# A gated linear-attention block and a bilinear FFN on one core: weights assembled as integers, and the order of the beginning

## The chip, the core and the metric

The kernel runs on one core of a Trainium2 chip. A core has TensorE (PE: matrix products), VectorE (DVE), ScalarE (ACT), GpSimd (POOL) and SyncE (SP), each with an instruction queue of its own that is worked off in order; they wait for each other through semaphores. The metric is the device time in microseconds, as the median of three runs.

## The reference

Four sequences (B = 4) of 768 tokens with 8 heads of 48 channels go through a gated recurrence, and its output through a bilinear feed-forward layer:

```python
f = 1.0 / (1.0 + np.exp(-f_logit))
for t in range(S):
    state = f[:, :, t, :, None] * state + np.einsum('bhd,bhe->bhde', k[:, :, t], v[:, :, t])
    y[:, :, t] = np.einsum('bhd,bhde->bhe', q[:, :, t], state)
x = y.transpose(0, 2, 1, 3).reshape(B * S, H * D)      # 3072 x 384
out = (x @ w_a) * (x @ w_b) @ w_out                    # 384 -> 1536 -> 384
```

q, k, v and f_logit are float32. The weights are float64: w_a, w_b and w_out reach the kernel as raw 64-bit words, 14 MB in all.

## The kernel before

**Attention.** The work is cut into 16 units: four heads and 384 tokens (BLK) each. Units 0 and 1 make the first block of 384 tokens (block 0), units 2 and 3 the second (block 1). A unit's f, k, q and v stand in one of three sets of buffers; unit 3 reuses unit 0's set. `front(u)` prepares a unit: ScalarE takes two sigmoids of f, one for `inv` and one in place; POOL scales `inv`; VectorE scans the running products of f and of the reciprocal gates (L242, L252) and multiplies them into q and k (L253, L254). These generators advance one step with each `next`. Then, on TensorE: `scores(u)` (24 products of k and q, masked by VectorE at L299), `turn(u)` (six transposes of k, copied by ScalarE as kT at L312), `within(u)` (scores times v), `gains(u)` (k times v; VectorE sums them into states, L343 and L345), `across(u)` (states times q). ScalarE copies y from PSUM at L396, and five DMAs move it into xT, the transposed input of the feed-forward layer (L410). y has one buffer only, so the next unit's copies wait for these DMAs.

**Feed-forward.** `up(blk, ft)` multiplies one block with 128 columns of w_b and of w_a: 3 + 3 matrix products, shown as x6 + x6 rows, L426. `product()` then lets ScalarE copy the b half (L441) and VectorE multiply it with the a half (L446). `down` multiplies three blocks of tokens with w_out in seven products instead of eight; its rows are L478 and L483.

**Weights.** The weights come in 20 pieces of up to 768 columns a partition: w_b and w_a alternate, then w_out. `load_weights` starts a piece's DMA into one of four raw buffers. `from_double` makes float32 of it, with two handles: `begin(n)` runs the first part of pieces up to n, `end(n)` the last. In the first part ScalarE takes the absolute value of the high words (scaled, so that the exponent fits), their sign, and the sign as a bit; POOL limits the value. The last part is four passes on VectorE (L188, L192, L194, L195), which shift the value into place, join the sign, cut out the power of two, scale the low words by it and add them. `up(0,0)` needs the first pieces of w_b and w_a, and the program makes its second product wait for the following w_b piece too; the later ups follow in the same manner.

**Order.** The whole program stands under a manual schedule: each engine takes its instructions in the order of the calls. From "with tc.manual_schedule()" on, the beginning is written out by hand, up to `up(0, 4)`; then the list `rest` begins with `up(1, 0)` and goes on in a loop, with the later units' parts queued beside it. Loads of all kinds and most xT DMAs leave through SP's queue, the others of the first two units through ScalarE's.

Of the kernel before, what the change touches and what calls it, by code (L numbers as in the profile page):

```python
# [78 lines left out]
def by_quotients(ctx, tc, q, k, f_logit, v, moe_w_a, moe_w_b, moe_w_out, out, ident, weights, bad):  # L79
# [7 lines left out]
    NJ = BLK // SUB  # L87
    NTG = BLK // 128
    NU = B * NH * NQ
    NBLK = B * NH  # L90
    NSET = 3

    fixedp = ctx.enter_context(tc.tile_pool(name="fixed", bufs=1))
# [21 lines left out]
    ones = fixed([128, 1], "ones")  # L115
    less = fixed([128, 1], "less")
    sign = fixedp.tile([128, PIECE], BF16, tag="sign", name="sign")
    bits = [fixedp.tile([128, PIECE], U32, tag=f"bit{i}", name=f"bit{i}") for i in range(3)]
# [7 lines left out]
    def load_unit(u, names="fkqv"):  # L126
        if u >= NU:
            return
        b, half, qd = unit(u)
        t = sets[u % NSET]  # L130
        cols = slice(half * BLK, half * BLK + BLK)
        for nm, src in (("f", f_logit), ("k", k), ("q", q)):
            if nm not in names:
                continue
            heads = src[b].rearrange("(n two) d s -> two d n s", two=2)
            for par in range(2):
                nc.sync.dma_start(out=t[nm][R * par:R * par + D], in_=heads[par][:, 2 * qd:2 * qd + 2, cols])
        if "v" in names:
            nc.sync.dma_start(
                out=t["v"].rearrange("s n c x -> s n (c x)"),  # L140
                in_=v[b, 2 * qd:2 * qd + 2, :, half * NC:half * NC + NC].rearrange("n s c two d -> s n (c two d)"),
            )

    def pieces():
# [5 lines left out]
        for ft in range(0, NFT, 2):  # L150
            rows = moe_w_out[ft * 128:(ft + 2) * 128]
            yield w_out[:, ft:ft + 2], rows.rearrange("(k p) c -> p k c", p=128), (2, DM)

    todo, raws, going = list(pieces()), [], []
    ended = [0]

    def load_weights(n=1):
        for _ in range(n):
            if len(raws) == len(todo):
                return  # L160
            dst, src, (k, m) = todo[len(raws)]
            raw = dst
            if src.dtype != FP32:
                raw = raw_pool.tile([128, PIECE], mybir.dt.uint64, tag="raw", name="raw")[:, 0:k * m]
                raw = raw.rearrange("p (k m) -> p k m", k=k)
            nc.sync.dma_start(out=raw, in_=src)
            raws.append(raw)

    def from_double(dst, raw, k, bit):


# [6 lines left out]
        bit, sgn = bit[:, 0:width], sign[:, 0:width]  # L178
        nc.scalar.activation(h, hi.bitcast(FP32), AF.Abs, scale=HI_SCALE)  # L179
        nc.scalar.activation(sgn, hi.bitcast(FP32), AF.Sign)  # L180

        nc.scalar.activation(
            bit.bitcast(U16).rearrange("p (n two) -> p n two", two=2)[:, :, 1], sgn, AF.Relu, scale=-32768.0
        )
        nc.gpsimd.tensor_scalar(h, h, HI_MAX, None, ALU.min)  # L185
        yield
        hu = h.bitcast(U32)
        nc.vector.scalar_tensor_tensor(  # L188
            out=hu, in0=hu, scalar=3, in1=bit, op0=ALU.logical_shift_left, op1=ALU.bitwise_or
        )  # L190

        nc.vector.tensor_scalar(bit, hu, 0xFF800000, None, ALU.bitwise_and)  # L192
        h, lo, power = (x.rearrange("p (k n) -> p k n", k=k) for x in (h, lo, bit.bitcast(FP32)))
        nc.vector.scalar_tensor_tensor(out=dst, in0=lo, scalar=2.0**-52, in1=power, op0=ALU.mult, op1=ALU.mult)  # L194
        nc.vector.tensor_tensor(dst, h, dst, ALU.add)  # L195
        yield

    def begin(n):

        while len(going) < min(n, len(todo)):  # L200
            i = len(going)
            dst, src, shape = todo[i]
            going.append(from_double(dst, raws[i], shape[0], bits[i % len(bits)]) if src.dtype != FP32 else iter(()))
            next(going[i], None)

    def end(n):

        while ended[0] < min(n, len(todo)):
            begin(ended[0] + 1)
            next(going[ended[0]], None)  # L210
            ended[0] += 1
            if ended[0] > 2:
                load_weights()
# [8 lines left out]

    live = {}
    xT = {}

# [3 lines left out]
    def front(u):  # L229

        t = sets[u % NSET]
        x = halves(t["f"])
        inv = sb2.tile([128, 2 * BLK], FP32, tag="inv", name="inv")
        nc.scalar.activation(inv, x, AF.Sigmoid, bias=less, scale=-1.0, accum_out=tails[:, u:u + 1])  # L234
        nc.scalar.activation(x, x, AF.Sigmoid)

# [3 lines left out]
        for n in range(2):  # L240
            c = slice(n * BLK, n * BLK + BLK)
            nc.vector.tensor_tensor_scan(x[:, c], x[:, c], none, math.exp(MIDDLE), ALU.mult, ALU.add)  # L242
        nc.vector.tensor_tensor(held[:, u], t["f"][:, :, BLK - 1], least, ALU.is_ge)
        yield

        start = sb2.tile([128, 2, NC - 1], FP32, tag="start", name="start")
        nc.vector.reciprocal(start, t["f"].rearrange("p n (c m) -> p n c m", m=C)[:, :, 0:NC - 1, C - 1])  # L247
        for n in range(2):
            for c in range(NC):
                w = slice(n * BLK + c * C, n * BLK + c * C + C)  # L250
                first = start[:, n, c - 1:c] if c else math.exp(-MIDDLE)
                nc.vector.tensor_tensor_scan(inv[:, w], inv[:, w], none[:, 0:C], first, ALU.mult, ALU.add)  # L252
        nc.vector.tensor_tensor(halves(t["q"]), halves(t["q"]), x, ALU.mult)  # L253
        nc.vector.tensor_tensor(halves(t["k"]), halves(t["k"]), inv, ALU.mult)  # L254
# [62 lines left out]
    def gains(u):  # L317
# [19 lines left out]
        before = live[u - NQ]["st"][NJ] if half else None  # L337
        live[u]["st"] = [before]
        for j in range(NJ - 1 if last else NJ):
# [6 lines left out]
            before = st[:, j]  # L346
            live[u]["st"].append(before)
        if not last:

            for n in range(2):  # L350
                end = t["f"][:, n, BLK - 1:BLK]
                nc.vector.tensor_scalar(before[:, n], before[:, n], end, math.exp(-MIDDLE), ALU.mult, ALU.mult)
# [19 lines left out]
    def across(u):  # L372
# [22 lines left out]
        for p, e, r, rows in (*whole, (1, R, 0, D), (1, 0, R, D)):  # L395
            nc.scalar.copy(y[r:r + rows, :, p], ps[p][e:e + rows, 0:BLK].rearrange("r (o m) -> r o m", m=SUB))  # L396
        y = y.rearrange("r (n c) p m -> r n (c p m)", n=2)
# [17 lines left out]

    HFT = NFT // 2
    products = {}
# [108 lines left out]
    def slot(u):  # L526
# [18 lines left out]
        yield  # L545
        next(nxt, None)
        yield

# [15 lines left out]

    with tc.manual_schedule():
        nc.scalar.preload_act_table_set("sigmoid_and_others")
        for x, value in ((less, -K_EXP), (zero, 0.0), (least, math.exp(MIDDLE - DECAY_MAX)), (ones, 1.0)):
            nc.gpsimd.memset(x, value)
        for n, x in (("f", 30.0), ("k", 0.0), ("q", 0.0)):
            for u in range(NSET):  # L570
                eng = nc.vector if n == "f" or n == "q" and u == 0 else nc.gpsimd
                eng.memset(sets[u][n], x)
        for ps in (ps_x, ps_y):
            nc.scalar.copy(ps[:, :, 0:BLK], zero.unsqueeze(1).broadcast_to((128, 2, BLK)))
        load_unit(0, "f")
        load_unit(1, "f")
        load_unit(0, "kqv")
        load_unit(1, "kqv")
        load_weights(2)
        load_unit(2)  # L580
        load_weights(2)


        fronts = [front(u) for u in range(2 * NQ + 1)]
        next(fronts[0])
        next(fronts[1])
        for bit in bits:
            nc.gpsimd.memset(bit, 0)
        make_identity(nc, ident)
        nc.gpsimd.memset(causal, 1.0)  # L590
        for p in range(2):
            half = causal[SUB * p:SUB * p + SUB]
            nc.gpsimd.affine_select(
                out=half, in_=half, compare_op=ALU.is_ge, fill=0.0, base=0, pattern=[[1, SUB]], channel_multiplier=-1
            )
        next(fronts[0])
        next(fronts[0])
        next(fronts[1])
        scores(0)
        turn(0, True)  # L600
        begin(2)
        next(fronts[1])
        within(0)
        gains(0)
        next(fronts[2])
        scores(1, True)
        turn(1, True)
        across(0)
        within(1, True)
        end(1)  # L610
        gains(1)
        across(1)
        for u in range(NQ):
            load_unit(u + NSET)
            load_weights()
        end(2)
        begin(3)


        next(fronts[2])  # L620
        next(fronts[2])
        scores(2)
        turn(2, True)
        next(fronts[3])
        begin(4)
        within(2)
        end(3)
        gains(2)
        up(0, 0)
        across(2)  # L630
        next(fronts[3])
        product()
        end(4)
        begin(5)
        up(0, 1)
        next(fronts[3])
        product()
        begin(6)
        scores(3)
        turn(3, True)  # L640
        up(0, 2)
        within(3)
        end(5)
        gains(3)
        product()
        end(6)
        begin(8)
        across(3)
        up(0, 3)
        product()  # L650
        up(0, 4)

# [16 lines left out]

        queue = [(2 * NFT - 4 + d, fronts[2 * NQ]) for d in (0, 0.9, 1.8)]  # L670
        for s in slots:
# [405 lines left out]
```

## Time and profile before

| what | us |
|---|---|
| median of 3 runs (lowest, highest) | 654.95 (654.27, 656.79) |
| the profiled execution, its span | 657.89, 656.1 |
| TensorE busy | 618.1 (94%) |
| VectorE busy | 327.7 (50%) |
| ScalarE busy | 174.9 (27%) |
| POOL busy | 68.9 (10%) |
| granted TensorE clock, mean over the span | 0.981 |

In the profile, a row of the timeline gives the start in the span, the time taken, the engine and the line, what was written from what, how many instructions are merged into it, and in brackets how long the engine had been idle before it and what ended that. The rows of slices give, for 40 equal stretches of the span, the busy tenths of each engine and the granted clock of TensorE in tenths. A window's row gives the busy time of each engine in a stretch, with the number of instructions, and the mean granted clock. A row named DMA_DIRECT2D is the issue of a transfer, not the transfer; the trace also has the time at which it landed.

### The profile page before, as it was taken

The numbers are of one execution on the slowest core, as the hardware profiler recorded it, in microseconds if no ns is written. First come the engines' busy times: TensorE is split into PE (matmuls) and PEld (weight loads), VectorE is DVE, ScalarE is ACT, GpSimd is POOL, SyncE is SP. The second block draws the span as 40 slices with busy tenths as digits, with TensorE's granted clock in tenths as the row PEclk, the third lists the DMA queues.
The fourth block names the chain that finished last, engine by engine and source line by source line (L and its number), as shares of the span: only waits on it lengthen the run. The fifth ranks groups of instructions, "written<-read, shape, count | busy, mean of one in ns | idle before, by whom it ended". The sixth has DMA issues, their size and how long they took to land.

```text
span 656.1 us, 12293 instructions
## 1 busy us (share of the span) xinstructions
PE 618.1 (94%) x5202; PEld 446.9 (68%) x5202; DVE 327.7 (50%) x610; ACT 174.9 (27%) x312; POOL 68.9 (10%) x57
## 2 busy tenths in 40 slices
PE   1667899999999999999999999999999999999996
PEld 1554555557898666966699666865689655865696
DVE  7878699995875345351443244443363121311241
ACT  3564677531321222122200312122200122011100
POOL 6232365410110000000000000000000000000000
PEclk9966999999999999999999999999999999999999
DMA  8688556100144124040210033140000000000000
GB/s 209 172 207 238 164 169 221 68 0 1 37 106 116 37 55 91 15 104 1 63 32 35 25 79 71 22 115 0 20 1 24 26 19 19 0 26 0 1 24 30
DMA packets 30209, 43.37 MB, mean 66 GB/s; under 512 B 3776, under 2 KB 24768, under 8 KB 30144
## 3 DMA queue, kind: packets, MB, share of 16 engines
q1 hardware_dynamic: 29856, 42.19, 23.7%
q8 instruction: 43, 0.70, 0.5%
q10 hardware_dynamic: 288, 0.30, 0.2%
q14 instruction: 22, 0.18, 0.1%
HBM read 33.03 MB, written 4.72 MB: 58 GB/s over the span
## 4 chain that ended last, share of the span: by engine, by line
PE 90%; DVE 5%; DMA 2%; ACT 1%; issue 1%; POOL 0%; ACTq 0%; SPq 0%; DVEq 0%
PE f L426 57%; PE f L483 24%; PE ps_x L283 2%; PE ps_y L363 2%; PE ps_y L384 2%; PE ps_x L329 1%; DMA xT<-y 1%; DVE inv L252 1%; PE ps_x L310 1%; DVE f_in L242 1%; PE f L310 1%; DVE k_in L254 1%; DMA f_in<-in_f_logit_dram 0%; DVE h L478 0%; DVE q_in L253 0%
## 5 line engine op out<-in xcount | busy, mean ns | idle before, releaser
L426 PE MATMUL f<-xT,w_a 128*128 128x384 f32 x576 | 203.6, 490 | 5.6 <-DVE start L247 4.6
L426 PE MATMUL f<-xT,w_b 128*128 128x384 f32 x576 | 205.7, 494 | 0.0
L426 PEld LDWEIGHTS f<-xT,w_a 128*128 128x128 f32 x576 | 110.1, 191 | 83.2 <-issue 6.4
L426 PEld LDWEIGHTS f<-xT,w_b 128*128 128x128 f32 x576 | 107.8, 191 | 70.4 <-issue 1.2
L446 DVE TENSOR_TENSOR ab<-f,b_sb 128x384 f32<-128x384 f32 x96 | 53.0, 554 | 180.4 <-PE f L426 130.1
L441 ACT COPY b_sb<-f 128x384 f32<-128x384 f32 x96 | 46.0, 479 | 238.9 <-PE f L426 225.8
L483 PE MATMUL f<-raw,h 128*128 128x192 f32 x432 | 73.7, 328 | 0.0
L483 PEld LDWEIGHTS f<-raw,h 128*128 128x128 f32 x432 | 70.2, 190 | 0.5
L483 PE MATMUL f<-w_out,ab 128*128 128x192 f32 x288 | 51.1, 327 | 0.9 <-DVE u L478 0.9
L237 POOL TENSOR_SCALAR inv<-inv 128x768 f32<-128x768 f32 x16 | 16.3, 1020 | 328.1 <-ACT inv L234 328.1
L185 POOL TENSOR_SCALAR h<-h 128x768 f32<-128x768 f32 (+1 forms) x20 | 44.0, 2202 | 61.3 <-ACT h L179 61.3
L483 PEld LDWEIGHTS f<-w_out,ab 128*128 128x128 f32 x288 | 47.4, 190 | 3.0 <-DVE u L478 1.2
L478 DVE TENSOR_TENSOR o<-f,u 128x192 f32<-128x192 f32 x36 | 12.9, 357 | 56.6 <-PE f L483 56.4
L283 PE MATMUL ps_x<-q_in,k_in 48*64 48x64 f32 x720 | 16.2, 238 | 22.1 <-DVE k_in L254 22.1
L283 PEld LDWEIGHTS ps_x<-q_in,k_in 48*64 48x64 f32 x720 | 14.6, 151 | 23.9 <-POOL causal L590 13.9
L242 DVE TENSOR_TENSOR_SCAN f_in<-f_in,zero 128x384 f32<-128x384 f32 x32 | 28.8, 941 | 3.1 <-POOL inv L237 3.1
L299 DVE TENSOR_TENSOR at<-ps_x,causal 128x768 f32<-128x768 f32 x15 | 14.4, 958 | 31.4 <-PE ps_x L283 31.3
L252 DVE TENSOR_TENSOR_SCAN inv<-inv,start,zero 128x128 f32<-128x128 f32 x64 | 27.5, 470 | 0.0
L345 DVE TENSOR_TENSOR st<-st,ps_x 128x96 f32<-128x96 f32 x80 | 20.3, 253 | 12.1 <-PE ps_x L329 9.6
L483 PE MATMUL f<-raw,ab 128*128 128x192 f32 x144 | 25.7, 328 | 0.0
L483 PE MATMUL f<-w_out,h 128*128 128x192 f32 x144 | 25.4, 326 | 0.0
L396 ACT COPY y<-ps_y 48x384 f32<-48x384 f32 (+1 forms) x45 | 21.4, 475 | 11.1 <-PE ps_y L384 10.0
(82 smaller groups left out, 477.1 us busy)
## 6 DMA issues: line engine op xcount, KB each, us to landing
f_in<-in_f_logit_dram SPq DMA_DIRECT2D x32, 144.0 KB, 3.2
k_in<-in_k_dram SPq DMA_DIRECT2D x32, 144.0 KB, 3.6
q_in<-in_q_dram SPq DMA_DIRECT2D x32, 144.0 KB, 3.9
v_in<-in_v_dram SPq DMA_DIRECT2D x16, 288.0 KB, 4.2
raw<-in_moe_w_out_dram SPq DMA_DIRECT2D x6, 768.0 KB, 4.3
out_dram<-o SPq DMA_DIRECT2D x24, 192.0 KB, 1.9
raw<-in_moe_w_b_dram SPq DMA_DIRECT2D x5, 768.0 KB, 7.4
raw<-in_moe_w_a_dram SPq DMA_DIRECT2D x5, 768.0 KB, 6.2
```

The lines of the kernel that those rows point to most:

```text
L185: nc.gpsimd.tensor_scalar(h, h, HI_MAX, None, ALU.min)
L237: nc.gpsimd.tensor_scalar(inv, inv, EXP_K, 1.0, ALU.mult, ALU.add)
L242: nc.vector.tensor_tensor_scan(x[:, c], x[:, c], none, math.exp(MIDDLE), ALU.mult, ALU.add)
L252: nc.vector.tensor_tensor_scan(inv[:, w], inv[:, w], none[:, 0:C], first, ALU.mult, ALU.add)
L283: nc.tensor.matmul(ps[h][SUB * p:SUB * p + SUB, o:o + SUB], lhsT=kf[r, tokens(n, c, p)], rhs=qf[r, tokens(n, c, p)], start=True, stop=True,)
L299: nc.vector.tensor_tensor(to, x, tri.broadcast_to((128, *lead, 2 * NC, SUB)), ALU.mult)
L345: nc.vector.tensor_tensor(st[:, j], before, new, ALU.add)
L396: nc.scalar.copy(y[r:r + rows, :, p], ps[p][e:e + rows, 0:BLK].rearrange("r (o m) -> r o m", m=SUB))
L426: nc.tensor.matmul(ps[nm], lhsT=w[:, kt, ft * 128:ft * 128 + 128], rhs=x[:, kt], start=kt == 0, stop=kt == NKT - 1,)
L441: nc.scalar.copy(b_sb, ps["b"])
L446: nc.vector.tensor_tensor(products[blk, part][:, :, i], a, b, ALU.mult)
L483: nc.tensor.matmul(to, lhsT=x[:, i], rhs=w[:, i], start=first and i == 0, stop=i == HFT - 1, skip_group_check=True)
```

## The change

It has four parts.

1. The low word of a double is no longer added in float32. ScalarE turns it into an integer-valued float in [2^23, 2^24] (one more pass: Identity with a scale of 2^-29 and a bias of 2^23), so that its bits hold the rounded low mantissa bits; the sign pass then overwrites that word's upper half with the sign bit. VectorE shifts the high value left by three and adds the two as 32-bit integers: two passes instead of four. In the built program the add is an instruction of its own kind, over twice as many 16-bit elements. `begin` can now run half of a piece's first part (`begin(4.5)`).
2. f of units 0 and 1 is loaded over all 64 rows of each half of the buffer (16 rows of the next head fill the rest), and needs no memset before it. The products of f of these two units stand in a buffer of their own, borrowed from the pool `ab`. POOL fills f with 30.0 before units 3 and 4 are loaded.
3. The raw words of pieces 4 and 5 go to two free buffers of the pool `ab`.
4. The beginning is reordered: the order of the loads (v late, k of unit 0 after the first w_b piece), `begin(3)` ahead of `scores(0)`, `turn` before `across` and `scores` of units 0 and 1, and unit 2 after `up(0,0)` instead of before it. Two of unit 0's and 1's y copies go to VectorE. `front`'s multiplications of q and k are a step of their own.

```diff
+    EARLY = (4, 5)
...
+                if len(raws) in EARLY:
+                    raw = ab_pool.tile([128, NTG * HFT * 128 // 2], mybir.dt.uint64, tag="ab", name="ab")
...
     def load_unit(u, names="fkqv"):
...
+        if u - NSET in FIRST and "f" in names:
+            nc.gpsimd.memset(t["f"], 30.0)
...
+            if nm == "f" and u in FIRST:
+                for par in range(2):
+                    row = ((b * H + 4 * qd + par) * D) * S + half * BLK
+                    rows = bass.AP(src.tensor, src.offset + row, [[S, R], [2 * D * S, 2], [1, BLK]])
+                    nc.sync.dma_start(out=t[nm][R * par:R * par + R], in_=rows)
...
     def from_double(dst, raw, k, bit):
...
         nc.scalar.activation(h, hi.bitcast(FP32), AF.Abs, scale=HI_SCALE)
+        nc.scalar.activation(bit.bitcast(FP32), lo, AF.Identity, bias=whole, scale=2.0**-29)
+        nc.gpsimd.tensor_scalar(h, h, HI_MAX, None, ALU.min)
+        yield
         nc.scalar.activation(sgn, hi.bitcast(FP32), AF.Sign)
...
-        nc.gpsimd.tensor_scalar(h, h, HI_MAX, None, ALU.min)
         yield
         hu = h.bitcast(U32)
-        nc.vector.scalar_tensor_tensor(
-            out=hu, in0=hu, scalar=3, in1=bit, op0=ALU.logical_shift_left, op1=ALU.bitwise_or
-        )
-        nc.vector.tensor_scalar(bit, hu, 0xFF800000, None, ALU.bitwise_and)
-        h, lo, power = (x.rearrange("p (k n) -> p k n", k=k) for x in (h, lo, bit.bitcast(FP32)))
-        nc.vector.scalar_tensor_tensor(out=dst, in0=lo, scalar=2.0**-52, in1=power, op0=ALU.mult, op1=ALU.mult)
-        nc.vector.tensor_tensor(dst, h, dst, ALU.add)
+        nc.vector.tensor_scalar(hu, hu, 3, None, ALU.logical_shift_left)
+        hu, bit = (x.rearrange("p (k n) -> p k n", k=k) for x in (hu, bit))
+        nc.vector.tensor_tensor(dst.bitcast(U32), hu, bit, ALU.add)
...
+            copy = nc.vector.tensor_copy if u in FIRST and p else nc.scalar.copy
...
```

The new beginning, without the memsets and with the lines of the old one left out:

```python
        load_unit(0, "f")
        load_unit(1, "f")
        next(fronts[0])
        load_unit(1, "q")
        load_unit(0, "q")
        load_unit(1, "k")
        load_weights()
        load_unit(0, "k")
        load_weights()
        patterns()
        next(fronts[0])
        load_weights()
        next(fronts[0])
        load_unit(1, "v")
        next(fronts[1])
        next(fronts[1])
        next(fronts[0])
        load_unit(0, "v")
        next(fronts[1])
        begin(3)
        load_unit(2, "k")
        load_unit(2, "f")
        scores(0)
        load_unit(2, "v")
        next(fronts[1])
        turn(0, True)
        within(0)
        gains(0)
        load_unit(NSET, "f")
        load_weights()
        next(fronts[2])
        turn(1, True)
        across(0)
        load_weights()
        scores(1, True)
        end(2)
        within(1, True)
        load_unit(2, "q")
        gains(1)
        across(1)
        load_weights()
        next(fronts[2])
        next(fronts[3])
        end(3)
        next(fronts[2])
        up(0, 0)
        next(fronts[2])
        load_unit(NSET, "q")
        begin(4.5)
        load_weights()
        product()
        load_unit(NSET, "v")
        end(4)
        scores(2, True)
        up(0, 1)
        next(fronts[3])
        load_unit(NSET + 1, "q")
        end(5)
        load_unit(NSET, "k")
        end(6)
        within(2)
        load_unit(NSET + 1, "f")
        load_unit(NSET + 1, "k")
        turn(2, True)
        load_weights()
        gains(2)
        load_unit(NSET + 1, "v")
        next(fronts[3])
        next(fronts[3])
        product()
        begin(7)
        up(0, 2)
        product()
        across(2)
        up(0, 3)
        begin(8)
        scores(3)
        turn(3, True)
        within(3)
        gains(3)
        across(3)
        up(0, 4)
        end(7)
        product()
        product()
        end(8)
```

## The prediction

> **What bounds the kernel now.** First the page's rows of slices, 16.4 us each.
>
> ```profile
> PE   1667899999999999999999999999999999999996
> DVE  7878699995875345351443244443363121311241
> ACT  3564677531321222122200312122200122011100
> PEclk9966999999999999999999999999999999999999
> ```
>
> TensorE is the bound from the fifth slice on; before it, it idles while VectorE is nearly full, and its granted clock falls in slices 3 and 4. The timeline of TensorE says where its work stands.
>
> ```profile
> 13.91 1.68 PE L283 MATMUL ps_x<-q_in,k_in 48*64 48x64 f32 x48 [13.91 <-DVE k_in L254]
> ...
> 37.81 1.65 PE L283 MATMUL ps_x<-q_in,k_in 48*64 48x64 f32 x48 [7.97 <-DVE k_in L254]
> ...
> 43.27 2.65 PE L426 MATMUL f<-xT,w_b 128*128 128x384 f32 x6
> ...
> 55.41 4.18 PE L426 MATMUL f<-xT,w_a 128*128 128x384 f32 x6 [4.60 <-DVE start L247]
> ...
> 82.48 2.10 PE L426 MATMUL f<-xT,w_a 128*128 128x384 f32 x6
> ```
>
> 13.91 is scores(0), 37.81 scores(2), 43.27 up(0,0); the pair ending in the last row is up(1,0), done at 84.42. I use 84.42 as the checkpoint: all work after it has the same order in both kernels. The third row with a wait names L247, but the VectorE row just before it is L195, the last pass of a weight piece (54.30 to 55.26): that is what this up waited for. The windows split the time at those marks:
>
> ```profile
> 30.00:35.00 5.00, 0.00 (x0) 0.00 (x0) 4.86 (x12) 1.89 (x4) 0.00 (x0) 0.56 0.04 10
> 40.00:45.00 5.00, 5.00 (x97) 3.99 (x96) 4.83 (x8) 4.45 (x8) 2.02 (x2) 0.58 1.07 293
> 55.00:60.00 5.00, 4.37 (x10) 2.04 (x11) 5.00 (x11) 1.70 (x2) 2.24 (x1) 0.50 0.56 121
> ...
> 43.27:84.42 41.15, 34.09 (x313) 20.62 (x311) 30.22 (x49) 23.73 (x34) 14.79 (x8) 0.86 0.77 211
> 84.42:150.00 65.58, 65.58 (x205) 38.68 (x204) 63.99 (x83) 38.56 (x55) 25.95 (x13) 1.00 0.32 104
> ```
>
> (PE, PEld, DVE, ACT, POOL busy, then clock.) From 84.42 on TensorE has no idle time to win, though VectorE is full; everything is decided before. There TensorE is idle 7.06 us of 41.15 and runs at half clock in two stretches (0.50 to 0.58 in the rows).
>
> **Part 1, weights as integers.** Four VectorE passes become two. The old ones, of the piece that ended the 4.60 us wait, and the new ScalarE pass's nearest row:
>
> ```profile
> 51.23 0.95 DVE L188 SCALAR_TENSOR_TENSOR h<-h,bit 128x768 uint32<-128x768 uint32 x1
> 52.22 1.06 DVE L192 TENSOR_SCALAR bit<-h 128x768 uint32<-128x768 uint32 x1
> 53.31 0.96 DVE L194 SCALAR_TENSOR_TENSOR w_a<-raw,bit 128x768 f32<-128x768 uint32 x1
> 54.30 0.96 DVE L195 TENSOR_TENSOR w_a<-h,w_a 128x768 f32<-128x768 f32 x1
> ...
> 43.16 0.89 ACT L179 ACTIVATE h<-raw 128x768 f32<-128x768 f32 x1
> ```
>
> From 51.23 to 55.18 is 3.95 us, in other pieces 3.43. New: a shift, nearest row L192 (usually 0.56), 0.59 with the step to the next; and an integer add, which no row shows. Its nearest row is L195, 0.96. Against the change speaks the Trainium skill, "DVE: scalar operands, raw-bit mode, write accounting and state across instructions", Raw-bit mode: the lane's add is fp32, exact on raw integers only below 2^24. So a 32-bit add must go in halves, and the built program indeed writes a 256-column piece as 512 columns. Twice 768 elements at L195's rate would be about 1.8 us. I take 0.96, with 1.8 as the other end: a piece costs 1.55 (or 2.4) instead of 3.43. At 1.8 the sum below loses some 0.5 us (up(0,1)), since the other pieces stand under matmuls.
>
> ScalarE gets a fourth pass, start to start 0.8: 3.6 us a piece instead of 2.8, and 2.05 for half pieces. Later, each up has one piece and one b_sb copy: 3.13 + 0.82 = 3.95 us of ScalarE (82.68 to 85.81 in the trace, plus the pass) per 3.87 of TensorE. For 11 piece-equivalents that is under 1 us of lag; a copy may come 1.9 us late before its product does, so it costs nothing.
>
> **Part 2, f whole and loads reordered.** The first f load left at 1.74, behind VectorE's memset; ScalarE and POOL start at 0.79, so I take 0.85. SP's loads land one after another: 0.68 us per 48-row load (issued 3.60 to 5.01, landed 7.20 to 9.36), v 1.0, half weight pieces 1.3, whole ones 2.0. The f loads grow to 64 rows, 0.9 each. In the new order: f of both units 6.5, q1, q0, k1 10.5, w_b 11.8, k0 13.2, w_a 14.5, w_b's second piece 16.6, v1, v0 18.6, k2, f2 21.3, v2, f3 23.7, w_a's second piece 25.8. VectorE has finished f0's and f1's scans and unit 0's quotients by 12.0, but k0 lands at 13.2: its product ends at 14.1 and scores(0) starts at 14.3. Nothing is won at the first matmul; the gain of the early f is used up by k0's place in the queue.
>
> **Part 3, the reordered beginning, step by step.** begin(3) puts three pieces on ScalarE ahead of unit 0's two kT copies: w_b 11.8 to 13.9, w_a 14.5 to 16.6, then 3.6 to 20.2. The copies end at 21.1 (17.58 before), and gains(0) ends 21.75 (19.49 before). VectorE's state chain takes 1.75 (rows L343, L345): 23.6; turn(1) and across(0) end 24.6. The y copies, shared with VectorE, end 26.3; scores(1)'s masks 27.2; within(1), gains(1) 29.6; states 31.4; across(1) 31.6, against 29.85 now. Here the change is 1.8 us behind.
>
> Then it gains. Now the second y waits 4.89 us for the first y's DMAs (ScalarE L396) and is done at 34.1; then it is ready at 32.8. Its ScalarE-issued xT DMAs leave until 33.9 and land 3.0 later (the last one now took 3.04), 37.0. up(0,0) runs from 37.2 instead of 43.27; but unit 2's four steps, which stand before it now, come after. VectorE, meanwhile: f2's scans 34.5, a piece 36.2, quotients 38.5, q2 and k2 40.3. Those hide in up(0,0).
>
> TensorE's sum from 37.2 to the end of up(1,0): six ups at 3.87 (a clocked-up pair, 80.55 to 84.42), 23.2; units 2 and 3, each scores 0.86, turn 0.75, within 0.8, gains 0.67, across 0.82: 7.8; less 1.3 of up(0,0) that runs early, on the first third of xT: 29.7. Waits: kT2 0.7, unit 3's mask and states 0.6; up(1,0), now only one up behind across(3) instead of two. Its xT needs 1.5 us of copies, five SP issues at 0.6 and 2.1 to land: across(3) ends about 63, ready 68.8, TensorE there 67.6, so 1.2. Together 2.5.
>
> Clock: TensorE idles from 31.6 to 37.2 and starts slow. The Trainium skill, "TensorE: Matmul & The Clock Gate", What's actually happening, has full rate return after about 3.4 us of sustained work, which at half speed loses 1.7. The rows say longer: work resumed at 37.81 and 55.41, the clock rose near 44.2 and 64.7, so 6.4 and 9.3 us, the second with a 0.2 us gap in it. Up(0,0) is dense, so I take 5.5 us, a loss of 2.8; by the rule the result would be 1.1 us lower, by the longer row 1.9 higher.
>
> 37.2 + 29.7 + 2.5 + 2.8 = 72.2, against 84.42: 12.2 us. The profiled execution took 657.89 (span 656.1, 1.8 around it), the median of the runs is 654.95; executions differ by that much, and I take the gain off the median: 654.95 - 12.2 = **642.8**.
>
> The two weight pieces loaded early, into product buffers that are free then, cost nothing: their raw words land about 31 and 37 (47.55 and 53.86 before), and ScalarE reaches them at 40 and 44. up(0,2), at 49.4, waits for the first of them, put together by 48.9; landing 10 us later it would eat that cover and hold up(0,2) by some 0.5. POOL loses three bit memsets (2.09 us) and gets three f memsets of 0.7, idle around both. The split step of each unit's front runs its halves in succession later on: nothing.
>
> **The rivals.** (1) The new chain slips: kT0 stands behind a weight load that must land at 16.6, and xT behind DMAs that share engines with weight loads (one now took 8.08 us behind them). 2 to 4 us late moves all: 645 to 647. (2) The clock stays low: a gap in each window, at scores(2), kT2 or the states, as at 59.8. Half clock until about 52 would lose 7.5 instead of 2.8: 647.5. For it speaks the 9.3 us case; against it, VectorE has slack at each of those points. (3) Slower: ScalarE becomes the bound. Should the new pass, integer in and strided, cost not 0.82 but x, each later step takes 3.13 + x against 3.87. With 11 pieces there, six more ahead of copies in the beginning and some 2 us that buffers absorb, 17(x - 0.74) - 2 reaches 12.2 at x = 1.6; at 2.0 the kernel would take about 662. The rows of L179 and L180 with the same stride (0.89) speak against it. (4) It does nothing: early waits merely move, and up(1,0) ends where it does now, 655. Against it, 5 us of waits and 5 of half clock have named causes here that go.
>
> **How the numbers follow.** Expected course 0.68, (1) 0.14, (2) 0.09, (4) 0.05, (3) 0.04. A measurement tells about 0.5% (3.3 us) from no change: below 651.7 lie the first three, 0.91; 0.05 within; 0.04 slower. The likeliest's own range is 639.5 to 645.5 (clock 1.9 up or 1.1 down, chain 1 to 2 either way); with (1) and most of (2) it reaches to 648.5.
>
> **What would show it.** scores(0) near 14; kT0 copied only after 20; across(1) ending after 31; up(0,0) at about 37 at half clock, full clock by 44; no TensorE wait of over 2 us between 40 and 72; up(1,0) done near 72; the integer add near 1 us and the new Identity pass near 0.85; from there the same rows, 12 us earlier. Wrong it would be with loads landing later than 0.68 us apart, a long wait at kT0 or xT, or ScalarE setting the pace of the ups.

## The result: 649.3 us, less than half of the gain that was predicted

The changed kernel takes 649.33 us (median of 4 runs, 648.95 to 650.63) against 654.80 before: a ratio of 0.9914, 95% interval 0.9889 to 0.9940. The forecast was 642.8, its range ended at 648.5. A later measurement gave 648.74 (6 runs, 647.99 to 650.09) against 657.01 for the kernel before, ratio 0.9879 (0.9857 to 0.9902); that too lies outside the range. The kernel after repeats well; the kernel before scatters from 654.3 to 658.7, and the gain with it, from 5.5 to 8.3 us.

The profiled execution took 649.68 us (span 647.9). The page's rows of slices, as shown for before:

```profile
PE   0859899999999999999999999999999999999996
DVE  6778345587774427161642345352444021311241
ACT  6577599632221322211201222122200212011100
PEclk9969999999999999999999999999999999999999
```

TensorE now has its idle time and its slow clock in the first slices alone; VectorE's full stretch is gone (busy 289.7 us instead of 327.7), ScalarE has more to do there (187.0 instead of 174.9). The timeline of TensorE for the same steps:

```profile
15.56 1.68 PE L308 MATMUL ps_x<-q_in,k_in 48*64 48x64 f32 x48 [15.56 <-DVE start L271]
...
38.12 1.65 PE L451 MATMUL f<-xT,w_b 128*128 128x384 f32 x2 [5.62 <-DVE w_b L211]
40.91 1.62 PE L451 MATMUL f<-xT,w_b 128*128 128x384 f32 x2 [1.15 <-DMA xT<-y]
42.32 4.04 PE L451 MATMUL f<-xT,w_a 128*128 128x384 f32 x6
46.29 0.93 PE L308 MATMUL f<-q_in,k_in 48*64 48x64 f32 x48
...
74.75 0.88 PE L451 MATMUL f<-xT,w_b 128*128 128x384 f32 x2 [0.51 <-DMA xT<-y]
75.47 2.10 PE L451 MATMUL f<-xT,w_a 128*128 128x384 f32 x6
```

15.56 is scores(0); 31.59 (not shown) to 46.29 is up(0,0), cut in three by waits; scores(2) follows it. The last row is the end of up(1,0), so the checkpoint lies at 77.40, the start of the next row; 72.2 was predicted, 84.42 stood before. The 4.60 us wait in the middle of up(0,1) is gone. The long waits are now inside up(0,0): 5.62 us for the third piece of weights, then 1.15 us for the last part of xT. The windows (PE, PEld, DVE, ACT, POOL busy, then clock):

```profile
35.99:46.23 10.24, 6.96 (x10) 3.03 (x10) 7.09 (x13) 9.54 (x13) 5.69 (x3) 0.50 1.00 308
46.23:77.40 31.17, 28.89 (x441) 18.34 (x441) 20.43 (x40) 18.64 (x29) 7.54 (x5) 1.00 0.70 179
77.40:150.00 72.60, 72.60 (x276) 43.39 (x275) 40.49 (x62) 49.52 (x71) 27.57 (x14) 1.00 0.33 105
```

One stretch at half clock instead of two, just over up(0,0), and full clock from there on.

Why up(0,0) came late is told by VectorE's and ScalarE's timelines around the second y and by the DMA view of 24 to 42 us (last column: median us from issue to landing):

```profile
33.43 1.14 DVE L422 COPY y<-f 48x384 f32<-48x384 f32 x2 [1.74 <-DMA xT<-y]
34.60 1.81 DVE L266 TENSOR_TENSOR_SCAN f_in<-f_in,zero 128x384 f32<-128x384 f32 x2
...
36.52 0.55 DVE L209 TENSOR_SCALAR h<-h 128x768 uint32<-128x768 uint32 x1
37.11 0.96 DVE L211 CUSTOM_DVE_ANT_0 w_b<-h,bit 128x1536 uint16<-128x1536 uint16 x1
```

```profile
33.40 0.97 ACT L422 COPY y<-f 48x384 f32<-48x384 f32 x2 [7.72 <-DMA xT<-y]
34.66 1.81 ACTq L436 DMA_DIRECT2D xT<-y  x3
```

```profile
xT<-y SPq DMA_DIRECT2D x4, 72.0 KB, 2.2
...
xT<-y ACTq DMA_DIRECT2D x2, 72.0 KB, 4.9
xT<-y ACTq DMA_DIRECT2D x2, 48.0 KB, 2.2
xT<-y ACTq DMA_DIRECT2D x2, 24.0 KB, 5.1
```

The second y waits for the DMAs of the first (one buffer), and they are late: SP issues the load of piece 4 at 27.68, ScalarE its last xT transfer at 28.23; the load lands at 33.05, the 24 KB transfer at 33.30. The same happens again: piece 5's load issued at 35.25, the last xT transfer (72 KB) at 35.85; they land at 40.45 and 40.78. In this execution the transfers issued ahead of the weight loads took 2.2 us (the rows of 72 KB on SP's queue and of 48 KB). The shift and the integer add of a piece are the two rows at 36.52 and 37.11.

### The profile page after: what moved, and what is told of

The parts are those of the page before. It is cut to its first block, busy times and chain, and to the rows that moved or that the text cites. A ratio compares the mean times of both kernels' runs of the same rounds, so it can differ in the third digit from the quotient of the medians.

```text
span 647.9 us, 12250 instructions
## 1 busy us (share of the span) xinstructions
PE 614.6 (95%) x5202; PEld 442.0 (68%) x5202; DVE 289.7 (45%) x572; ACT 187.0 (29%) x328; POOL 65.6 (10%) x58
## 4 chain that ended last, share of the span: by engine, by line
PE 92%; DMA 4%; ACT 1%; SPq 1%; DVE 0%; ACTq 0%; issue 0%; DVEq 0%
PE f L451 58%; PE f L508 26%; DMA xT<-y 2%; PE ps_y L409 2%; PE ps_y L388 2%; PE ps_x L354 2%; PE ps_x L308 2%; PE ps_x L335 1%; DMA q_in<-in_q_dram 1%; DMA raw<-in_moe_w_a_dram 1%; SPq L145 0%; PE f L335 0%; ACTq L436 0%; DVE y L422 0%; ACT bit L204 0%
## 5 line engine op out<-in xcount | busy, mean ns | idle before, releaser
L261 POOL TENSOR_SCALAR inv<-inv 128x768 f32<-128x768 f32 x16 | 18.0, 1123 | 333.1 <-ACT inv L257 333.0
L200 POOL TENSOR_SCALAR h<-h 128x768 f32<-128x768 f32 (+1 forms) x20 | 40.7, 2035 | 51.4 <-ACT h L197 49.7
L308 PE MATMUL ps_x<-q_in,k_in 48*64 48x64 f32 x672 | 13.6, 226 | 15.6 <-DVE start L271 15.6
L266 DVE TENSOR_TENSOR_SCAN f_in<-f_in,zero 128x384 f32<-128x384 f32 x28 | 25.2, 940 | 0.0
L339 ACT COPY kT<-ps_x 128x768 f32<-128x768 f32 x12 | 9.6, 800 | 51.3 <-PE ps_x L335 51.3
```

Of the source, the lines that this page charges most:

```text
L261: nc.gpsimd.tensor_scalar(inv, inv, EXP_K, 1.0, ALU.mult, ALU.add)
L266: nc.vector.tensor_tensor_scan(F[:, c], F[:, c], none, math.exp(MIDDLE), ALU.mult, ALU.add)
L308: nc.tensor.matmul(ps[h][SUB * p:SUB * p + SUB, o:o + SUB], lhsT=kf[r, tokens(n, c, p)], rhs=qf[r, tokens(n, c, p)], start=True, stop=True,)
```

## Experiments

### Each part alone

Before with the integer conversion alone (the new `from_double`, no memset of the bits, the old order), and after with the four-pass conversion (the new order alone):

```diff
+        nc.scalar.activation(bit.bitcast(FP32), lo, AF.Identity, bias=whole, scale=2.0**-29)
...
-        nc.vector.scalar_tensor_tensor(
-            out=hu, in0=hu, scalar=3, in1=bit, op0=ALU.logical_shift_left, op1=ALU.bitwise_or
-        )
...
-        nc.vector.tensor_tensor(dst, h, dst, ALU.add)
+        nc.vector.tensor_scalar(hu, hu, 3, None, ALU.logical_shift_left)
...
+        nc.vector.tensor_tensor(dst.bitcast(U32), hu, bit, ALU.add)
```

> The kernel before with the integer conversion alone (two VectorE passes and one more ScalarE pass a piece; order, loads and buffers as before). If the conversion is what makes the changed kernel faster: 3 to 5 us under the kernel before, 650 to 652, with the wait of 4.6 us before up(0,1)'s second half down to some 2.2 us, and the 0.9 us wait near 165 us gone. If the order makes it: under 2 us of gain, 653 or more.

> The changed kernel with the old conversion of weights (four VectorE passes, no extra ScalarE pass, POOL clears the bit buffers), everything else as changed. If the conversion makes the gain: 4 us or more slower than the changed kernel, 653.5 or above, because up(0,0) then waits for its piece till about 42 and every product of unit 2 and 3 comes later. If the order makes it: within 1.5 us of the changed kernel.

Measured, beside 19 runs of before at 655.56: the conversion alone 651.29 (650.99 to 652.86), ratio 0.9936 (0.9912 to 0.9959); the order alone 655.63 (14 runs, 653.76 to 658.98), ratio 0.9992 (0.9975 to 1.0010). So the conversion is worth some 4 us on its own, and the order nothing on its own. With the conversion alone, the wait before up(0,1)'s second half shrank to 2.62 us (2.2 were expected), but the wait of 0.92 us late in the kernel, which was expected to go, stayed. The timeline of TensorE of the order alone:

```profile
32.27 2.25 PE L412 MATMUL f<-q_in,st 48*48 48x64 f32 x40 [2.85 <-DVE st L371]
...
42.22 1.62 PE L454 MATMUL f<-xT,w_b 128*128 128x384 f32 x2 [2.72 <-DMA xT<-y]
...
52.44 3.66 PE L454 MATMUL f<-xT,w_a 128*128 128x384 f32 x6 [2.14 <-DVE w_a L214]
```

The old conversion's four passes, moved ahead, hold up VectorE: across(1) waits 2.85 us for states that stand behind two half pieces, and a later up waits for a piece again. In between, up(0,0) waits for xT, where I had expected it to wait for its weights. So this order wins nothing with the long conversion; what it would win with its late xT transfers mended was not tried. With both parts, 649: the order then adds about 2 us.

### The kernel before again: how much there was to win

> The kernel before, unchanged, for a second profile. The prediction took its checkpoint (end of up(1,0) at 84.42 us) from an execution of 657.9 us, some 3 us over the median, and took the gain off the median. If that execution's surplus lay before the checkpoint (a longer stretch at half clock, a later transfer), an execution near 655 ends up(1,0) at 81 to 82, and about 3 us of the predicted 12.2 never were there to win. If the surplus lay behind the checkpoint, up(1,0) ends at 84 again.

> The changed kernel, unchanged, on the same chip as the two runs beside it: 649 to 650 us, as the yardstick for them; up(1,0) ends at 77 to 78.5.

Both are unchanged kernels. This execution of before, a single one, took 654.73 us. Its timeline of TensorE (the row after up(1,0)), and its window where the first execution had its second slow stretch:

```profile
81.31 2.10 PE L426 MATMUL f<-xT,w_b 128*128 128x384 f32 x6
```

```profile
54.45:64.69 10.24, 9.60 (x76) 5.61 (x78) 9.07 (x14) 3.69 (x6) 2.29 (x2) 0.85 0.60 170
```

up(1,0) ends at 81.31 instead of 84.42, as the first expectation had it. The clock was 0.85 over the stretch in which the execution that I had costed stood at 0.50, and the second y had waited 3.36 us instead of 4.89 (ScalarE's timelines, the costed execution first):

```profile
32.15 1.96 ACT L396 COPY y<-f 48x384 f32<-48x384 f32 x4 [4.89 <-DMA xT<-y]
```

```profile
29.54 1.95 ACT L396 COPY y<-f 48x384 f32<-48x384 f32 x4 [3.36 <-DMA xT<-y]
```

So 3.1 of the 12.2 us were a surplus of the costed execution over this one, which ran at the median that I took the gain off. How often before runs like this is not shown: its mean granted clock, 0.988, is above that of all 41 runs of before measured with the experiments (0.976 to 0.986), and in those the clock does not tell fast from slow (654.71 us at 0.982, 658.30 at 0.986). What makes before scatter stays open. After again: 648.74, up(1,0) at 76.28, both just under what was expected.

### The xT transfers behind the weight loads

Three kernels, all from after. The first moves the load of piece 4 behind across(1) and gives the last xT transfer of unit 1 to SP, where it stands ahead of both loads; the second makes the first edit alone, the third the second alone.

```diff
         across(0)
-        load_weights()
...
         across(1)
-        load_weights()
+        load_weights(2)
...
-                    queue = nc.scalar if u < NQ and (n + h) % 2 else nc.sync
+                    queue = nc.scalar if u < NQ and (n + h) % 2 and (u, n) != (1, 1) else nc.sync
```

> The changed kernel with two weight loads (pieces 4 and 5) issued only after both units' xT transfers, and with one of unit 1's ScalarE-issued xT transfers moved to SP, so that none leaves behind a weight load. Theory Q (the first ups wait because y and xT transfers share the transfer engines with weight loads): unit 1's y copies start near 31.7 us instead of 33.4, the last third of up(0,0) at about 36.5 to 37.5 instead of 40.9, and the time falls by 3 to 4.3 us, to about 645.5. Rival C (the slow clock after the idle stretch is what costs; the transfers only fill time that would be idle anyway): the transfers land earlier, but less than 1 us is gained, 648.5 to 649.5.

> After, with the load of piece 4 alone moved from ahead of scores(1) to behind across(1), next to that of piece 5; the xT transfers stay on the queues they were on. Theory (each small transfer issued after a weight load lands behind it): the y of unit 1 is copied at 32 instead of 33.4, as its buffer is free 3 us earlier, but the last xT transfer, issued by ScalarE beside the two weight loads, still lands behind at least one of them, 4 to 6 us after its issue, at 38 to 40; up(0,0)'s last third starts there: 647 to 649 us. Rival (only the first of the two delays counts): the last xT transfer lands within 3 us, and the time is that of the kernel with both edits, 646.4.

> After with one line changed: the last xT transfer of unit 1 is issued by SyncE, ahead of piece 5's load in the same queue, instead of by ScalarE beside it; piece 4's load stays where it is. Theory (this transfer, landing 5 us after its issue behind piece 5's load, is what up(0,0)'s last third waited for): it lands by 37.5 to 38, up(0,0)'s last third starts right behind its second at 39.5 or earlier, 647 to 648 us; with piece 4's load moved too it was 646.4. Rival (piece 4's load ahead of unit 0's transfers is the delay that counts): no better than after, 648.7 to 649.5.

Both edits: 646.39 (5 runs, 644.65 to 647.48), ratio 0.9860 (0.9835 to 0.9885). Piece 4 alone: 649.02 (648.57 to 649.51). The last transfer alone: 648.11 (647.03 to 649.13). After stood at 649.33 and 648.74, and its ten runs (647.99 to 650.63) do not overlap with those of both edits. The gain of both is 2.4 to 2.9 us: a little under the 3 to 4.3 of the theory, well over the rival's 1. The kernel with 14 filler products below contains both edits too, and was measured beside after: 645.86 against 648.74. Piece 4 alone won nothing beside after; the last transfer alone lies between its two forecasts, and its runs overlap with after's. The timelines of TensorE from up(0,0)'s second part on, of both edits:

```profile
36.09 2.93 PE L451 MATMUL f<-xT,w_b 128*128 128x384 f32 x4 [4.58 <-DVE w_b L211]
38.81 2.44 PE L451 MATMUL f<-xT,w_a 128*128 128x384 f32 x6
41.18 0.93 PE L308 MATMUL f<-q_in,k_in 48*64 48x64 f32 x48
...
72.23 2.10 PE L451 MATMUL f<-xT,w_b 128*128 128x384 f32 x6
```

of piece 4 alone:

```profile
37.73 1.65 PE L451 MATMUL f<-xT,w_b 128*128 128x384 f32 x2 [3.19 <-DVE w_b L211]
40.55 1.62 PE L451 MATMUL f<-xT,w_b 128*128 128x384 f32 x2 [1.17 <-DMA xT<-y]
```

and of the last transfer alone:

```profile
38.40 2.93 PE L451 MATMUL f<-xT,w_b 128*128 128x384 f32 x4 [6.34 <-DVE w_b L211]
```

There are two delays side by side, and each covers for the other. Piece 5's load makes the last xT transfer late (40.55: landed 40.41, 4.94 after its issue). Piece 4's load makes the second y late, and on VectorE that y stands ahead of unit 2's products of f and of the weight piece, so the piece is late too (38.40). Take one away and the other still holds up(0,0) to 38.4 or 40.6; take both away and it goes on at 36.09, and scores(2) starts at 41.18 instead of 46.29. These are single executions. That of both edits was the fastest of its five (644.65), 5.0 us under the profiled one of after, while the medians differ by about half of that; 1 us of the difference was there already when across(1) ended (30.7 against 31.7). In this the expectation for piece 4 alone was right about the time, and wrong about y: it was copied at 33.03, not 32, as TensorE came to across(1) late in that execution (30.71).

### The slow clock

After with 44 products of the identity with itself between across(1) and up(0,0), results unused; then the kernel of both edits with 14 of them and, besides, the third weight piece put together ahead of unit 2's running products.

```diff
+    def filler(n):
+        for _ in range(n):
+            nc.tensor.matmul(ps_y[:, 0, 0:128], lhsT=ident, rhs=ident, start=True, stop=True, skip_group_check=True)
...
         across(1)
+        filler(14)
         load_weights(2)
+        end(3)
         next(fronts[2])
         next(fronts[3])
-        end(3)
         next(fronts[2])
```

> The changed kernel with 44 throw-away products of the identity with itself on TensorE between across(1) and up(0,0), about 5.5 us of them, so that it doesn't idle there (extra work, the outputs don't depend on it). Rival C: the granted clock stays full through 40 us, the last two thirds of up(0,0) take 2.6 us instead of 5.3, and the time falls by 2.5 us or more, to about 646.7. Theory Q: the clock stays up too, but the last third of up(0,0) still starts at 40.9 behind the transfer; the gain is the 2.6 us of half clock and no more.

> The kernel with both loads moved (646.4 us), with two more edits: the third weight piece is put together ahead of unit 2's running products on VectorE, and 14 products of the identity with itself (results unused, about 3.2 us at full clock) keep TensorE busy between across(1) and up(0,0). Without them up(0,0)'s second part waited until 36.1 for that piece, 1.0 after its xT, and ran at half clock. Theory (VectorE's chain to k2 at 40.5 bounds the step behind): up(0,0) starts its second part at 35.1 to 35.5 at full clock and is done by 39, but scores(2) starts only at 40.3 to 40.6: 645.5 to 646. Rival (slow clock is the limit): scores(2) starts by 39.5, 644 to 645.

The first took 650.10 us (648.22 to 652.11), no better than after, and is no clean test of the clock. The granted clock was 1.00 from 31.0 to 46.0, as wanted, but I had sized the filler badly: it took 10.1 us instead of 5.5 and ended at 41.9, a microsecond after the last xT, and the parts of up(0,0) that had run at 31.6 and 38.1 were now behind it. up(0,0) ran at full clock, and was done at 45.91 instead of 46.29. Had the filler ended with the transfer it would have been 44.9 (an estimate), 1.4 us under after. With the first two parts left in their places, the last eight products at full clock would end near 43.5, 2.8 us under after; that too is an estimate, and no run shows it. The second took 645.86 (644.18 to 646.77), ratio 0.9826 (0.9802 to 0.9851). Its timeline of TensorE:

```profile
34.02 1.76 PE L451 MATMUL f<-xT,w_b 128*128 128x384 f32 x4
36.16 0.88 PE L451 MATMUL f<-xT,w_b 128*128 128x384 f32 x2 [0.39 <-DMA xT<-y]
36.88 2.10 PE L451 MATMUL f<-xT,w_a 128*128 128x384 f32 x6
41.47 1.04 PE L308 MATMUL f<-q_in,k_in 48*64 48x64 f32 x48 [2.48 <-ACT bit L199]
42.44 3.64 PE L451 MATMUL f<-xT,w_b 128*128 128x384 f32 x6
```

up(0,0) starts 2 us earlier, runs at full clock and is done by 38.9, but scores(2) does not come earlier (41.47; 41.18 without): TensorE waits 2.48 us. The row names ScalarE, but what scores(2) reads is unit 2's k, and VectorE's product for it ran from 40.27 to 41.22. With the transfers out of the way VectorE's chain to that k is what holds scores(2), neither the clock nor xT; without the filler that k was ready at 40.50, 0.7 us before scores(2). But the wait had a price behind it: the clock fell to half, and up(0,1) took 5.8 us instead of 4.1.

```profile
43.05:46.46 3.41, 3.41 (x6) 1.69 (x6) 3.41 (x5) 3.38 (x5) 2.37 (x2) 0.50 1.08 319
```

So the filler moved the slow work from up(0,0) to up(0,1), as much as there had been (3.41 us of it; 3.40 without the filler), and the total is that of the kernel without it (646.39). What a full clock throughout would give, no run shows.

### The beginning: ScalarE's order and f

The kernel of both edits with the third piece's ScalarE passes and unit 2's sigmoids behind the copies of kT and of y instead of ahead of them; the same with the filler, the early third piece and all of the first y copied by ScalarE; and after with f of units 0 and 1 in 48-row loads behind memsets, as before.

```diff
-        begin(3)
+        begin(2)
...
-        next(fronts[2])
         turn(1, True)
         across(0)
+        next(fronts[2])
+        begin(3)
```

> The kernel with both loads moved (646.4 us), with the third weight piece's four ScalarE passes and unit 2's two sigmoids behind the copies of kT0, kT1 and y0 instead of ahead of them. Theory (the beginning is set by the order of ScalarE's work, as the prediction's 'Here the change is 1.8 us behind' says): kT0 is copied by 19.3 instead of 21, gains(0) ends at 20.3, across(1) at 28.4 to 29 instead of 30.6, and all behind it follows: 644 to 644.8 us. Rival (the xT transfers and VectorE's chain from there on take it up): across(1) is earlier, scores(2) is not, 646 to 646.5.

> All in one: the two loads moved, the conversion of the third piece ahead of unit 2's running products, 14 identity products as filler (645.9 us with these), then ScalarE's order as in the run beside it, and both halves of y0 copied by ScalarE so that VectorE's chain to k2 is 1.1 us shorter. Theory (VectorE's chain to k2 sets scores(2)): k2 done at 37.5 to 38.5 instead of 41.2, 642.5 to 643.5 us. Rival (transfers set it): above 645.

> After with unit 0's and 1's f loaded as before, in four loads of 48 rows behind memsets on VectorE, instead of two of 64 rows. By the prediction nothing is won by the whole f at the first product, since k0's place in the queue sets scores(0): scores(0) at 15.5 to 16, as with it (15.6), and 648.7 to 650 us. If the early f counts, scores(0) comes at 16.5 or later and the time is above 650.5.

Measured 648.17 (647.16 to 649.73), 647.39 (646.06 to 648.01) and 650.11 (648.49 to 650.45). The first two missed both of their forecasts: 1.8 and 1.5 us worse than the kernels that they were made from. The timeline of TensorE of the first:

```profile
19.35 1.53 PE L388 MATMUL ps_y<-at,v_in 64*48 64x64 f32 x48 [0.50 <-DMA v_in<-in_v_dram]
20.63 1.06 PE L354 MATMUL ps_x<-v_in,kT 64*48 64x48 f32 x48
...
26.70 0.51 PE L308 MATMUL f<-q_in,k_in 48*64 48x64 f32 x20 [2.48 <-issue]
```

kT0 was copied by 19.4, as expected, but within(0) stands ahead of gains(0) and waits for v of unit 0, which lands at 19.2; gains(0) ended at 21.7 instead of 21.9 in the kernel of both edits. So the wait for kT0, which the prediction had put down to ScalarE's order, was covered by v's place in SP's queue. Then TensorE stood still for 2.48 us in scores(1), waiting for nothing that the profile shows (2.41 us in the second kernel), and across(1) ended at 33.5 instead of 30.7. That these gaps are what made the two kernels slower is argued from the timelines, not tested. f in halves: scores(0) at 15.48 with it and 15.56 without, and a time whose runs overlap with after's. The whole f wins nothing at scores(0), as predicted.

## Why the prediction was wrong

Its steps against the first profile of after:

| step | predicted | measured |
|---|---|---|
| scores(0) starts | 14.3 | 15.56 |
| kT0 copied | 21.1 | 21.3 |
| across(1) ends | 31.6 | 31.7 |
| second y copied | 32.8 | 34.6 |
| third piece put together | 36.2 | 38.1 |
| last xT lands | 37.0 | 40.8 |
| from there to the end of up(1,0) | 35.0 | 36.5 |
| shift and add of a piece | 1.55 | 1.55 |
| new ScalarE pass, start to start | 0.8 | 0.9 |

**The step that failed** is "Its ScalarE-issued xT DMAs leave until 33.9 and land 3.0 later (the last one now took 3.04), 37.0", and with it "The two weight pieces loaded early ... cost nothing". I asked when the words of these pieces would be needed, and not what their loads, issued 0.6 us ahead of small transfers, would do to those. Both xT groups landed behind them: +1.8 us at the second y, +2.0 at the last transfer, 3.8 together, all of it on the path of this execution. Moving them out of the loads' way gave back 2.4 to 2.9 us in the medians; behind them VectorE's chain to unit 2's k comes next. Rival (1) named this mechanism ("xT behind DMAs that share engines with weight loads"), and its 2 to 4 us were right, though its 645 to 647 stood on the same base as the forecast; the chance of 0.14 was too small, with the 8.08 us row in hand.

**The base was wrong by nearly as much.** "executions differ by that much, and I take the gain off the median": the gain was worked out inside an execution that was 3 us slower than the median. A gain counted against such an execution contains its surplus. Beside the second execution, that lay where the change was to win (the second stretch at half clock, the wait of the second y). Against the other execution of before, the predicted 72.2 gives 81.31 - 72.2 = 9.1 us, so 645.6, inside the range. The gap closes: 642.8 + 3.1 (base) + 3.8 (transfers) + 1.5 (products) - 1.0 = 650.2, against 649.7 in this execution.

**The rest of the sum stood the test** in the kernel of both edits, in part by luck. In its profiled execution up(1,0) ends at 72.23, predicted 72.2, and the time is 644.65: the costed 657.89 less 12.2 and less the 1.0 below is 644.7. But it was the fastest of five, up(0,0) was done 1.4 us before the sum's 42.6, and the steps behind it took 31.0 us instead of 29.6.

**The 1.5 us** are sizes: ups that alternate with other products take 4.0 to 4.2 us and not the 3.87 of the dense pair (some 1.1 us over the five), the steps of units 2 and 3 some 0.6 more than summed; the waits came to 2.3 instead of 2.5. **The 1.0 us** that came in addition lie behind the checkpoint, where I had seen nothing to win: the wait of 0.92 us ahead of a `down` product at 165.6 (162.5 in the second profile of before) is no longer in after. The kernel with the conversion alone still has it (158.5), the one with the order alone does not, so the order takes it away; by what was not tried.

**What was right:** the price of the conversion. The add cost what its nearest row said, 0.96 us. It writes 1536 16-bit elements for 768 words, which fits the limit of 2^24 that the Trainium skill ("DVE: scalar operands, raw-bit mode, write accounting and state across instructions", Raw-bit mode) gives for an fp32 add on raw integers; the doubled price that I had drawn from it did not come. VectorE is 38 us less busy, the 4.60 us wait went, ScalarE did not become the bound (rival 3), one slow stretch went (against rival 2). The loss at half clock behind 40.91 was 2.8 us, as predicted; neither filler turned it into time.

**The clock's 5.5 us** to full rate were a middle value of cases that have one pattern behind them. In after it took 8.1 us (38.12 to 46.23), in the kernel of both edits 3.4 (36.09 to 39.49). The stretches at half clock last 3.41 us or a multiple of it: 6.83 in the kernel of both edits, 10.24 in after, 17.07 in its second execution (27.18 to 44.25). Cut each of these into pieces of 3.41 us from its start, and it ends with the first piece that TensorE filled; so do the two stretches of before. The windows of these last pieces, of both edits (its whole stretch, with the 3.40 us of work in the last piece), of after, and of the two stretches of before:

```profile
32.66:39.49 6.83, 3.40 (x6) 1.89 (x7) 6.76 (x13) 6.14 (x9) 3.13 (x2) 0.50 0.81 269
```

```profile
42.82:46.23 3.41, 3.41 (x6) 1.35 (x4) 0.33 (x1) 3.35 (x5) 2.27 (x1) 0.50 1.05 325
```

```profile
40.79:44.21 3.42, 3.42 (x91) 2.96 (x91) 3.32 (x4) 3.23 (x7) 1.23 (x2) 0.50 1.05 334
61.27:64.69 3.42, 3.42 (x20) 2.48 (x13) 2.98 (x4) 0.96 (x2) 0.00 (x0) 0.50 0.94 293
```

Work that resumes inside a piece, or stops in it, did not count here, and so 3.4 us of work became 8.1 in after, and 6.4 and 9.3 in before. This agrees with the Trainium skill ("TensorE: Matmul & The Clock Gate", What's actually happening), whose 3.4 us are a window that runs on by itself and does not start with the work; that is what the 5.5 left out. What exactly counts is not settled: in the kernel with the order alone TensorE was busy all through 32.50 to 35.91, with across(1)'s small products for the most part, and stayed at half clock, while 2.99 us of work between 38.44 and 41.85 ended the stretch in the kernel with kT first.

What stays open: scores(0) was 1.3 us late (the scans ended at 13.3 instead of 12.0, k0 landed at 13.83 instead of 13.2, its product took 1.26), which did not show at across(1); why before scatters; and the gaps without a named cause in TensorE, below.

## What to carry to other kernels

Before a load is moved earlier, list the small transfers that are issued within its flight time, on another queue too, and who waits for them; issue those first, or behind them the load. Take a gain off the execution in which it was counted, or profile twice: where the clock has slow stretches, the stretch that a change removes may be one that the median never had. Two delays that end at the same place hide each other, and an edit that removes one alone looks useless, as piece 4's load did here.

## What was not expected of the hardware

- A small transfer issued on ScalarE's queue just after a large load on SP's did not pass it. The 24 KB of 28.23 landed at 33.30, 0.25 us behind the 768 KB that were issued 0.55 us before it; the 72 KB of 35.85 landed 0.33 us behind theirs; with the loads moved away such transfers took 2.3 and 2.6 us in the median. The DMA views of after show where the time went. From 37.2 to 39.2, with the transfer of 35.85 under way, only SP's queue (q1) moves packets; ScalarE's (q10) does from 39.2 to 40.5:

```profile
q1 hardware_dynamic: 251, 0.51, 82.3%
```

```profile
q1 hardware_dynamic: 227, 0.43, 90.5%
q10 hardware_dynamic: 64, 0.07, 15.7%
```

  The Trainium skill, "DMA: Bandwidth & Descriptors", Queues, rings and completion order, has each DMA engine take turns, packet by packet, between the queues that it has work for. That alone would have let the 72 KB through earlier; whether they had reached the engines before 39.2 no view shows, so the cause of the delay stays open. To be issued first by a hair was not enough either: in the second execution of after, ScalarE's transfer of 26.38 left 0.01 us ahead of the load and took 6.4 us.
- TensorE has an idle stretch of 1.4 to 1.8 us ("issue") between scores(1) and within(1) in the kernels of the new order (1.38 in after), up to 2.48 where kT stands first; in the second profile of before there is one of 0.49 ahead of 24.0, and one of 1.25 ahead of 41.9. In after a 16 KB packet of the queue that carries instructions moved in that gap (the DMA view of 26.0 to 27.6):

```profile
q8 instruction: 1, 0.02, 3.4%
```

  Instructions that came late would be one reading; the Trainium skill, "Runtime: NRT & Kernel Launch", Instruction fetch mechanics, calls such fetches mostly hidden. Against it speaks the second execution of after: its gap of 1.80 us (24.5 to 26.3) has no packet of that queue in it. No run separates the causes.
